# Where the states and the x transposes of a cross-attention and maxout-FFN kernel stand in the order of work

## The chip, the cores and the metric

The kernel runs on one core of a Trainium2 chip. The metric is device time in microseconds (us). Five runs of the kernel before gave a median of 156.76 us (156.15 to 157.01).

A core has five engines with their own instruction queues: TensorE (PE: matmuls and transposes into psum), VectorE (DVE), ScalarE (ACT), GpSimd (POOL) and SyncE (SP, which here only issues DMAs). Each executes its queue strictly in the order written; semaphores make one wait for another.

## The reference

```python
def _attn_ref(x, state):                  # x: (8, 8, 512, 64), state: (8, 8, 32, 64)
    scores = scale * np.matmul(x, state.transpose(0, 1, 3, 2))
    a = softmax(scores)                    # over the 32 states
    xread = np.matmul(a, state)
    scores2 = scale * np.matmul(state, x.transpose(0, 1, 3, 2))
    a2 = softmax(scores2)                  # over the 512 rows of x
    sread = np.matmul(a2, x)
    return np.concatenate([xread, sread], axis=2)

x = attn_out.transpose(0, 2, 1, 3).reshape(B * S, H * D)   # 4352 tokens of 512
h = np.maximum(np.maximum(x @ w1, x @ w2), x @ w3)         # 768 wide
out = h @ w_out
```

Every x row of a batch attends to the 32 states of its head, every state to the 512 rows; the concatenated result goes through a feed-forward net whose hidden layer is the maximum of three products.

## The kernel before, in words

Everything is in bf16 with fp32 accumulation. Instead of computing xread and then x @ w, the kernel multiplies the states of a batch by the weights first (G, by `g_cols`, `g_piece`, `g_front`, `g_back`); the hidden layer is then the softmax weights times G. For a batch b the steps are:

- x of the batch is loaded by a GpSimd DMA (`load_x`) and transposed to xT. For batches 0 to 2 that is done on PE in two halves of eight 128x128 transposes each (`x_transpose(b, g, copy)`, lines 157 to 167: transposes L164 into a psum tile, copied out to xT at L167 by the engine named). From batch 3 on one DMA transpose on SP's queue does it (`x_transpose_dma`, L171).
- `scores` (L185) multiplies xT by the states, which lie block by block in a tile `bds[k]` for the pair of batches 2k and 2k + 1; ScalarE takes the exp (L190, tile e). `softmax` sums and inverts on VectorE (L197, L199) and multiplies on GpSimd (L200, tile a).
- a is transposed to aT (on PE for batches 0 to 2, `a_transpose`, L211 and L212; later by DMA, L216).
- `sread` (L230) computes the second attention from e and x; its result is DMA-transposed into `ats` by `late_transposes` (L238). ats is read only in the last batch's iteration, by `s_maxout`.
- `x_maxout(b, m)` (L332) does one of six blocks of the hidden layer: three products of two matmuls each into three psum tiles; ScalarE copies the first (t0, L336), VectorE takes the maximum with the second (L339) and with the third (L340, tile ht). Each step frees one psum tile.
- `ffn_out(b, j)` (L370) multiplies by w_out, six matmuls; ScalarE copies out (L373); the output is stored by DMA (L382).

The state tile of a pair is made in three steps. `load_st` loads it (L58). `states_cast` (L135) casts it and doubles it into `st[k]`. `states(k, copy)` transposes it, on PE for the first two pairs (L142) and by a DMA on SP's queue for the others (L145, tile stT), and puts it into `bds[k]` by two copies (L148).

Psum is shared by two groups of buffers: tag "pw" (four buffers: the products of `x_maxout`, `ffn_out`, the transposes, `sread`, the short G pieces) and tag "two" (two larger ones: scores and G). A new tile waits for whoever last read the buffer that it gets.

The order of the work is written out by hand. The lines 391 to 470 are a first phase, in which batches 0 and 1 are worked on together and batch 2 is prepared. The loop at line 473 then does, for each batch b from 2 on, its six `x_maxout` blocks, and between them, in slots, the attention of batch b + 1 and the output of batch b - 1. In slot 2 of odd n = b + 1 the states of the next pair are transposed and placed (lines 480 and 481). In `g_cols` a copy can be deferred; it is then issued inside the next `x_maxout`, behind its t0.

The part of the first phase around the change, before it: the cast of pair 1 (line 444), the states of pair 1 and the x transposes of batch 2 (446 to 448), x_maxout(0, 5), g_cols of batch 1, x_maxout(1, 3), scores and softmax of batch 2 (449 to 453), the waiting ats transposes and the transpose of x of batch 3 (454, 455), output and G work, load_x(5), and the casts of pairs 2 and 3 (460 to 462).

Of the kernel before, what the change touches and what calls it, by code (L numbers as in the profile page):

```python
# [9 lines left out]
BF16 = mybir.dt.bfloat16  # L10
# [5 lines left out]
def kernel(  # L16
# [14 lines left out]
    nc = tc.nc  # L31

    B, H, S, D = x.shape
# [15 lines left out]
    data = ctx.enter_context(tc.tile_pool(name="data", bufs=1))  # L49
    wpool = ctx.enter_context(tc.tile_pool(name="weights", bufs=1))  # L50
    work = ctx.enter_context(tc.tile_pool(name="work", bufs=2))
    pp = ctx.enter_context(tc.tile_pool(name="pp", bufs=2, space=bass.MemoryType.PSUM))
    ctx.enter_context(tc.manual_schedule())
    dve, act, pool = nc.vector.tensor_copy, nc.scalar.copy, nc.gpsimd.tensor_copy
# [31 lines left out]
    ident = const.tile([128, 128], BF16, name="ident")  # L86
# [13 lines left out]
    def m_cols(t, m):  # L100
        c = [m0 <= m < m1 for m0, m1 in chunks].index(True)
        f = (m - chunks[c][0]) * 128
        return w_slices(t, c)[:, :, :, f:f + 128]
# [25 lines left out]
    def bd(b, h):  # L129
        return bds[b // 2][:, b % 2, h]  # L130

    st = [data.tile([128, 4, 2, D], BF16, name=f"st{k}") for k in range(B // 2)]

    def states_cast(k, cast):
        cast(out=st[k], in_=st_f[k].unsqueeze(2).to_broadcast((128, 4, 2, D)))  # L135

    def states(k, copy):

        if k < 2:
            p = pp.tile([128, 4, 128], BF16, tag="pw", bufs=4, name="pt")  # L140
            for t in range(4):
                nc.tensor.transpose(p[:, t, :], st[k][:, t].rearrange("p c d -> p (c d)"), ident)  # L142
        else:
            p = data.tile([128, 4, 128], BF16, name=f"stT{k}")
            nc.sync.dma_start_transpose(out=p, in_=st[k].rearrange("p t c d -> p (t c d)"))  # L145
        for c in range(2):
            r = slice(64 * c, 64 * c + 64)
            copy(out=bds[k][r, :, :, c, :].rearrange("p b h (q t) -> p (b h) q t", t=4),  # L148
                 in_=p[r].rearrange("p t (k q) -> p k q t", q=8))


    xT, e, a, aT, G, ht, osb = {}, {}, {}, {}, {}, {}, {}
# [1 line left out]
    def new(d, b, shape, name, bufs=2):  # L154
        d[b] = work.tile(shape, BF16, tag=name, bufs=bufs, name=name)

    def x_transpose(b, g, copy):

        if g == 0:
            new(xT, b, [128, H, 2, 128], "xT", bufs=3)  # L160
        p = pp.tile([128, HS, 2, 128], BF16, tag="pw", bufs=4, name="pxt")
        for s in range(HS):
            for jj in range(2):
                nc.tensor.transpose(  # L164
                    p[:, s, jj, :],
                    xv[b][:, 2 * s + g, 2 * jj:2 * jj + 2, :].rearrange("p j d -> p (j d)"), ident)
        copy(out=xT[b].rearrange("p (s g) j t -> p g s j t", g=2)[:, g], in_=p)  # L167
# [5 lines left out]
    def scores(b, g0, g1):  # L173
        n = g1 - g0
        if g0 == 0:
            new(e, b, [128, J, 2, HS, Ns], "e")
        if n == 2:
            p = pp.tile([128, J, n, HS, Ns], F32, tag="two", name="ps")
        else:
            p = pp.tile([128, J, n, HS, Ns], F32, tag="pw", bufs=4, name="psh")  # L180
        for jj in range(2):
            for g in range(g0, g1):
                for s in range(HS):
                    h = 2 * s + g
                    nc.tensor.matmul(  # L185
                        p[:, 2 * jj:2 * jj + 2, g - g0, s, :], xT[b][:, h, jj, :],
                        bd(b, h).rearrange("p c n -> p (c n)"),
                        start=(g == g0 and s == 0 and (n == 2 or jj == 0)),
                        stop=(g == g1 - 1 and s == HS - 1), skip_group_check=True)
        nc.scalar.activation(out=e[b][:, :, g0:g1], in_=p, func=AF.Exp, scale=scale)  # L190

    def softmax(b, g0, g1, mul):
        n = g1 - g0
        if g0 == 0:
            new(a, b, [128, J, 2, HS, Ns], "a")
        den = work.tile([128, J, n, HS], F32, tag=f"den{n}", name="den")
        nc.vector.reduce_sum(out=den, in_=e[b][:, :, g0:g1], axis=AX.X)  # L197
        rden = work.tile([128, J, n, HS], F32, tag=f"rden{n}", name="rden")
        nc.vector.reciprocal(out=rden, in_=den)  # L199
        mul(  # L200
            out=a[b][:, :, g0:g1].rearrange("p j g s n -> p j (g s) n"),
            in0=e[b][:, :, g0:g1].rearrange("p j g s n -> p j (g s) n"),
            in1=rden.rearrange("p j g s -> p j (g s)").unsqueeze(3).to_broadcast((128, J, n * HS, Ns)))
# [40 lines left out]
    def flush_copies():  # L244
        while copies_due:
            copies_due.pop(0)()
# [30 lines left out]
    def g_cols(b, ms, copies=(act, act), defer=(False, False)):  # L277
        flush_copies()
        for m, copy, wait in zip(ms, copies, defer):
            if m == 0:  # L280
                new(G, b, [128, 2, NM * 384], "G", bufs=3)
            p = pp.tile([128, 2, 512], F32, tag="two", name="pg")
            pv = p[:, :, 0:384].rearrange("p g (i f) -> p g i f", i=3)
            for s in range(HS):
                for g in range(2):
                    nc.tensor.matmul(  # L286
                        pv[32 * s:32 * s + 32, g], bd(b, 2 * s + g)[64 * g:64 * g + 64, g, :],
                        m_cols(w_sb, m)[64 * g:64 * g + 64, s],
                        start=True, stop=True, tile_position=(64 * g, 32 * s))

            def place(m=m, pv=pv, copy=copy):
                copy(out=m_cols(G[b], m), in_=pv)  # L292

            if wait:
                copies_due.append(place)
            else:
                place()
# [27 lines left out]
    def maxout(b, m, n, lhs, rhs, nk):  # L325
        if m == 0:
            new(ht, b, [128, NM, n], "ht", bufs=4)
        pw = []
        for i in range(3):
            p = pp.tile([128, 512], F32, tag="pw", bufs=4, name=f"pw{i}")  # L330
            for k in range(nk):
                nc.tensor.matmul(p[:, 0:n], lhs(i, k), rhs(k), start=(k == 0), stop=(k == nk - 1))  # L332
            pw.append(p)
        t0 = work.tile([128, 512], BF16, tag="t0", name="t0")
        t1 = work.tile([128, 512], BF16, tag="t1", name="t1")
        nc.scalar.copy(out=t0[:, 0:n], in_=pw[0][:, 0:n])  # L336
        if copies_due:
            copies_due.pop(0)()
        nc.vector.tensor_max(t1[:, 0:n], t0[:, 0:n], pw[1][:, 0:n])  # L339
        nc.vector.tensor_max(ht[b][:, m, :], t1[:, 0:n], pw[2][:, 0:n])  # L340

    def x_maxout(b, m):
        maxout(b, m, 512,
               lambda i, k: m_cols(G[b], m)[:, k, i],
               lambda k: aT[b][:, :, k, :], 2)
# [41 lines left out]
    def late_transposes():  # L387
        while late:
            late.pop(0)()
# [51 lines left out]
    x_maxout(0, 3)  # L441
    g_cols(0, (4, 5), defer=(False, True))
    x_maxout(1, 2)
    states_cast(1, pool)
    x_maxout(0, 4)
    states(1, act)
    x_transpose(2, 0, dve)
    x_transpose(2, 1, act)
    x_maxout(0, 5)
    g_cols(1, (4, 5), defer=(False, True))  # L450
    x_maxout(1, 3)
    scores(2, 0, 2)
    softmax(2, 0, 2, nc.gpsimd.tensor_mul)
    late_transposes()
    x_transpose_dma(3)
    ffn_out(0, 0)
# [2 lines left out]
    ffn_out(0, 1)  # L459
    load_x(5)  # L460
    for k in range(2, B // 2):
        states_cast(k, pool)
    x_maxout(1, 5)
    a_transpose(2, 0, act)
    a_transpose(2, 1, dve)
# [7 lines left out]
    for b in range(2, B):  # L473
        n = b + 1
        slots = [[] for _ in range(NM)]
        if n < B:
            slots[0].append(lambda: scores(n, 0, 2))
            slots[1].append(lambda: softmax(n, 0, 2, nc.gpsimd.tensor_mul))
            slots[2].append(lambda: a_transpose_dma(n))
            if n % 2 and n + 1 < B:  # L480
                slots[2].append(lambda: states((n + 1) // 2, pool))
            if n + 2 < B:
                slots[2].append(lambda: x_transpose_dma(n + 2))
            slots[5].append(late_transposes)
            if n + 3 < B:
                slots[0].append(lambda: load_x(n + 3))
        else:
            for m in range(NM):
                slots[m].append(lambda m=m: s_maxout(m))
        slots[1].append(lambda: g_back(b))  # L490
        if n < B:
            slots[4].append(lambda: sread(n))
            slots[4].append(lambda: g_front(n))
        for j, m in enumerate((1, 2, 4, 5)):
            slots[m].insert(0 if m > 2 else len(slots[m]), lambda j=j: ffn_out(b - 1, j))
        for m in range(NM):
            x_maxout(b, m)
            for f in slots[m]:
                f()
# [36 lines left out]
```

## Time and profile before

| | |
|---|---|
| profiled execution | 156.68 us, its span 154.8 us |
| PE busy | 146.3 us, 95% of the span |
| VectorE, ScalarE, GpSimd busy | 98.2, 93.9, 51.2 us |
| granted PE clock | full in all 40 slices |
| chain that ended last | PE 81%, ACT 6%, DMA 4%, POOL 3%, DVE 2% |
| costliest lines of the chain | L332 43%, L370 27% |
| GpSimd copies bd<-stT, L148 | 4 of 1.07 us; GpSimd waited 8.9 us in all for them |

In the profile's group lines stand the source line, the engine, the operation, the tile written and those read, the shape, the number of instructions, the busy time and the mean of one, and at last how long the engine stood idle before them and who ended that. In a timeline a row begins with its start, counted from the start of the span, and its length; rows of equal instructions are merged. In the chain of waits each row is a start, a length, and what the last-ending work was then held by.

### The profile page before, as it was taken

The page shows a single profiled execution, that of the slowest core. Times are in us where ns is not written, and L with a number is a line of the kernel's source. Part 1 is how long each engine was busy: PE and PEld are TensorE (multiplying, and loading weights), DVE is VectorE, ACT ScalarE, POOL GpSimd, SP SyncE. Part 2 cuts the span into 40 slices and gives each one's busy share as a digit, 9 for nine tenths or more (in the row PEclk, how much of TensorE's full clock was granted, in tenths as well). Part 3 has the DMA queues.
Part 4 walks back from the last instruction along what each step waited for, and adds up shares of the span by engine and source line. Part 5 has one row for each costly group of instructions (what it writes and reads, how often), then busy time and mean ns, then how long its engine had stood idle before and what let it go on. Part 6 is the DMA issues. An engine that isn't in the chain of part 4 may idle for free.

```text
span 154.8 us, 3467 instructions
## 1 busy us (share of the span) xinstructions
PE 146.3 (95%) x1373; PEld 72.5 (47%) x1389; DVE 98.2 (63%) x173; ACT 93.9 (61%) x145; POOL 51.2 (33%) x73
## 2 busy tenths in 40 slices
PE   6898999999999999999999999999999999999990
PEld 2455443544553445344534453445344556666450
DVE  4777958768617675767576757675767583565110
ACT  3275788897647656865686568656865637333340
POOL 8979793003731409160104250601060100100050
PEclk9999999999999999999999999999999999999999
DMA  3999999999299996989930893070307030110374
GB/s 119 206 180 188 195 197 165 239 201 171 112 130 126 269 198 153 251 112 238 114 135 0 161 225 135 2 207 8 135 12 196 16 132 0 68 70 0 140 239 168
DMA packets 36736, 21.72 MB, mean 140 GB/s; under 512 B 21968, under 2 KB 34384, under 8 KB 36720
## 3 DMA queue, kind: packets, MB, share of 16 engines
q0 software_dynamic: 17232, 15.08, 51.2%
q1 hardware_dynamic: 19344, 6.29, 23.0%
q8 instruction: 11, 0.18, 0.5%
q10 hardware_dynamic: 144, 0.13, 0.2%
q14 instruction: 5, 0.04, 0.1%
HBM read 15.20 MB, written 8.91 MB: 156 GB/s over the span
## 4 chain that ended last, share of the span: by engine, by line
PE 81%; ACT 6%; DMA 4%; POOL 3%; DVE 2%; issue 2%; POOLq 0%; ACTq 0%
PE pw L332 43%; PE po L370 27%; DMA w<-in_moe_w_dram 4%; PE pg L260 4%; PE psr L230 2%; ACT G L292 2%; POOL x L80 2%; PE ps L185 2%; ACT t L336 1%; ACT e L190 1%; PE pg L286 1%; POOL w L110 1%; PE ph L362 1%; DVE den L197 1%; PE pxt L164 1%
## 5 line engine op out<-in xcount | busy, mean ns | idle before, releaser
L332 PE MATMUL pw<-aT,G 128*128 128x512 bf16 x288 | 68.8, 379 | 0.7 <-ACT G L292 0.4
L339 DVE TENSOR_TENSOR t<-t,pw 128x512 bf16<-128x512 bf16 (+1 forms) x54 | 35.0, 649 | 30.8 <-ACT t L336 30.6
L370 PE MATMUL po<-wout,ht 128*128 128x512 bf16 x183 | 46.6, 379 | 0.9
L332 PEld LDWEIGHTS <-G 128*128 128x128 bf16 x288 | 27.1, 98 | 33.0 <-issue 2.7
L340 DVE TENSOR_TENSOR ht<-t,pw 128x512 bf16<-128x512 bf16 (+1 forms) x54 | 35.5, 658 | 6.0 <-DVE t L339 0.5
L373 ACT COPY osb<-po 128x512 f32<-128x512 f32 x33 | 19.3, 586 | 29.8 <-PE po L370 29.8
L336 ACT CAST t<-pw 128x512 bf16<-128x512 f32 (+1 forms) x54 | 30.5, 565 | 9.7 <-PE pw L332 9.0
L370 PEld LDWEIGHTS <-ht 128*128 128x128 bf16 x198 | 18.8, 98 | 23.8 <-issue 2.8
L200 POOL TENSOR_TENSOR a<-e,rden 128x1024 bf16<-128x1024 bf16 (+1 forms) x9 | 14.6, 1627 | 39.3 <-DVE rden L199 23.4
L267 ACT CAST G<-pg 128x1024 bf16<-128x1024 f32 x24 | 24.5, 1021 | 3.8 <-PE pg L260 3.2
L382 POOL DMA_DIRECT2D out_dram<-osb x14 | 8.0, 570 | 45.2 <-ACT osb L373 36.5
L197 DVE TENSOR_REDUCE den<-e 128x32 f32<-128x1024 bf16 (+1 forms) x10 | 9.9, 995 | 0.8 <-ACT e L190 0.8
L292 ACT CAST G<-pg 128x768 bf16<-128x768 f32 x11 | 8.7, 809 | 2.0 <-PE pg L286 2.0
L110 POOL DMA_DIRECT2D w<-in_moe_w_dram x12 | 9.1, 779 | 0.0
L332 PE MATMUL pw<-ats,w 128*128 128x256 bf16 x72 | 8.8, 273 | 0.0
L190 ACT ACTIVATE e<-ps 128x1024 bf16<-128x1024 f32 x6 | 6.1, 1024 | 3.8 <-PE ps L185 3.7
L332 PEld LDWEIGHTS <-w 128*128 128x128 bf16 x72 | 7.0, 98 | 2.1
L260 PE MATMUL pg<-w,bd 64*32 64x512 bf16 x192 | 7.5, 381 | 0.0
L126 PE MATMUL idle<-zero 128*128 128x512 bf16 x18 | 6.3, 480 | 1.2 <-DVE zero L85 1.2
L148 POOL COPY bd<-stT 64x512 bf16<-64x512 bf16 x4 | 4.3, 1071 | 9.0 <-DMA stT<-st 8.9
L185 PEld LDWEIGHTS <-xT 128*128 128x128 bf16 x128 | 4.9, 98 | 2.6 <-DVE xT L167 0.7
L70 POOL DMA_DIRECT2D x<-in_x_dram x6 | 5.4, 917 | 0.0
(54 smaller groups left out, 81.5 us busy)
## 6 DMA issues: line engine op xcount, KB each, us to landing
out_dram<-osb POOLq DMA_DIRECT2D x14, 512.0 KB, 3.1
x<-in_x_dram POOLq DMA_DIRECT2D x6, 512.0 KB, 9.6
w<-in_moe_w_dram POOLq DMA_DIRECT2D x6, 256.0 KB, 7.0
x<-in_x_dram POOLq DMA_DIRECT2D x3, 256.0 KB, 5.7
w<-in_moe_w_dram POOLq DMA_DIRECT2D x6, 128.0 KB, 6.6
wout<-in_moe_w_out_dram POOLq DMA_DIRECT2D x1, 768.0 KB, 10.8
x0f<-in_x_dram SPq DMA_DIRECT2D x1, 512.0 KB, 3.8
out_dram<-osb SPq DMA_DIRECT2D x1, 512.0 KB, 2.6
```

The costliest lines, as they stand in the source:

```text
L110: nc.gpsimd.dma_start(out=w_slices(w_sb, c)[:, :, i, :], in_=w[:, :, m0 * 128:m1 * 128])
L197: nc.vector.reduce_sum(out=den, in_=e[b][:, :, g0:g1], axis=AX.X)
L200: mul(out=a[b][:, :, g0:g1].rearrange("p j g s n -> p j (g s) n"), in0=e[b][:, :, g0:g1].rearrange("p j g s n -> p j (g s) n"), in1=rden.r ...
L260: nc.tensor.matmul(ps[g][32 * s:32 * s + 32], bd(b, 2 * s + g)[64 * g:64 * g + 64, g, :], w_sb[64 * g:64 * g + 64, s, c0:c1], start=True, ...
L267: copy(out=G[b][:, :, c0:c1], in_=p[:, :, 0:n])
L292: copy(out=m_cols(G[b], m), in_=pv)
L332: nc.tensor.matmul(p[:, 0:n], lhs(i, k), rhs(k), start=(k == 0), stop=(k == nk - 1))
L336: nc.scalar.copy(out=t0[:, 0:n], in_=pw[0][:, 0:n])
L339: nc.vector.tensor_max(t1[:, 0:n], t0[:, 0:n], pw[1][:, 0:n])
L340: nc.vector.tensor_max(ht[b][:, m, :], t1[:, 0:n], pw[2][:, 0:n])
L370: nc.tensor.matmul(p, ht[b][:, m, j * 128:(j + 1) * 128], wout_sb[:, m, :], start=(m == 0), stop=(m == NM - 1))
L373: act(out=o[:, j, :], in_=p)
```

## The change

- `states` is cut into `states_transpose(k, dma)` and `states_place(k, copy)`; `states(k, copy)` remains for pairs 0 and 1 and does both, on PE.
- The casts of pairs 2 and 3 (states of batches 4 to 7) stand right behind that of pair 1.
- Their DMA transposes are issued on SP's queue behind the softmax of batch 2, ahead of `late_transposes` and of the transpose of x of batch 3.
- Their placing copies on GpSimd stand where the casts were, behind load_x(5).
- The loop issues no states any more.
- The second half of the PE transposes of x of batch 2, with its ScalarE copy, moves behind x_maxout(0, 5) and g_cols(1, (4, 5)).

```diff
-    def states(k, copy):
-
-        if k < 2:
-            p = pp.tile([128, 4, 128], BF16, tag="pw", bufs=4, name="pt")
+    stT = {}
+
+    def states_transpose(k, dma):
+
+        if dma:
+            stT[k] = data.tile([128, 4, 128], BF16, name=f"stT{k}")
+            nc.sync.dma_start_transpose(out=stT[k], in_=st[k].rearrange("p t c d -> p (t c d)"))
+        else:
+            stT[k] = pp.tile([128, 4, 128], BF16, tag="pw", bufs=4, name="pt")
             for t in range(4):
-                nc.tensor.transpose(p[:, t, :], st[k][:, t].rearrange("p c d -> p (c d)"), ident)
-        else:
-            p = data.tile([128, 4, 128], BF16, name=f"stT{k}")
-            nc.sync.dma_start_transpose(out=p, in_=st[k].rearrange("p t c d -> p (t c d)"))
+                nc.tensor.transpose(stT[k][:, t, :], st[k][:, t].rearrange("p c d -> p (c d)"), ident)
+
+    def states_place(k, copy):
         for c in range(2):
             r = slice(64 * c, 64 * c + 64)
             copy(out=bds[k][r, :, :, c, :].rearrange("p b h (q t) -> p (b h) q t", t=4),
-                 in_=p[r].rearrange("p t (k q) -> p k q t", q=8))
+                 in_=stT[k][r].rearrange("p t (k q) -> p k q t", q=8))
+
+    def states(k, copy):
+        states_transpose(k, False)
+        states_place(k, copy)
...
     x_maxout(1, 2)
-    states_cast(1, pool)
+    for k in range(1, B // 2):
+        states_cast(k, pool)
     x_maxout(0, 4)
     states(1, act)
     x_transpose(2, 0, dve)
-    x_transpose(2, 1, act)
     x_maxout(0, 5)
     g_cols(1, (4, 5), defer=(False, True))
+    x_transpose(2, 1, act)
     x_maxout(1, 3)
     scores(2, 0, 2)
     softmax(2, 0, 2, nc.gpsimd.tensor_mul)
+    for k in range(2, B // 2):
+        states_transpose(k, True)
     late_transposes()
     x_transpose_dma(3)
...
     load_x(5)
     for k in range(2, B // 2):
-        states_cast(k, pool)
+        states_place(k, pool)
     x_maxout(1, 5)
...
             slots[2].append(lambda: a_transpose_dma(n))
-            if n % 2 and n + 1 < B:
-                slots[2].append(lambda: states((n + 1) // 2, pool))
             if n + 2 < B:
```

## The prediction

> **What bounds the kernel now.** I read four views in this order: the page's busy table, busy time by stretches cut at batch borders, the chain of work that ended last, and ScalarE's instructions in the stretch that the change rewrites.
>
> ```profile
> PE 146.3 (95%) x1373; PEld 72.5 (47%) x1389; DVE 98.2 (63%) x173; ACT 93.9 (61%) x145; POOL 51.2 (33%) x73
> ```
>
> The matrix engine is the bound on average; no other engine passes 63%. The average must be split, because the change works in one stage only. The stretches begin where the FFN of a batch starts (two columns matter: length and PE busy).
>
> ```profile
> 29.26:44.58 15.32, 14.73 (x163) 7.71 (x164) 10.32 (x19) 10.83 (x16) 4.60 (x5) 1.00 0.97 163
> 44.58:59.99 15.41, 15.31 (x147) 7.03 (x148) 10.49 (x18) 10.24 (x15) 5.11 (x5) 1.00 1.30 196
> 59.99:75.40 15.41, 15.30 (x148) 7.03 (x148) 10.72 (x19) 10.24 (x15) 4.87 (x6) 1.00 0.91 175
> 75.40:90.81 15.41, 15.30 (x148) 7.02 (x149) 10.72 (x19) 10.24 (x15) 5.13 (x5) 1.00 0.53 101
> 90.81:106.20 15.39, 15.29 (x147) 7.03 (x148) 10.70 (x19) 10.24 (x15) 2.99 (x3) 1.00 0.43 136
> ```
>
> The loop runs at 15.41, 15.41, 15.41 and 15.39 us per batch. The first and the third of these hold a state placement (states of batches 4 and 5, then 6 and 7), the others hold none, and they are equal: the placement costs the loop 0.00 to 0.02 us. Only the first phase has PE time to win: 15.32 - 14.73 = 0.59 us. There the chain of waits tells who sets the pace (start, us, what):
>
> ```profile
> 30.11 0.69 DVE ht L340
> 30.80 0.04 issue
> 30.84 1.46 PE pw L332 x6
> ...
> 33.35 0.59 ACT t L336
> 33.94 0.70 ACT G L292
> ...
> 34.71 1.03 ACT e L190
> 35.74 0.02 issue
> 35.77 1.23 DVE den L197
> ...
> 37.29 0.64 DVE t L339
> 37.93 0.04 issue
> 37.97 1.47 PE po L370 x6
> ```
>
> Two places, not one. PE waits near 30.5 for a psum buffer, which VectorE's second max frees at 30.80. From 33.35 to 37.97 the chain leaves PE: ScalarE's t0, its G copy and its exp of batch 2, then VectorE's row sum, reciprocal and max, which frees the buffer for ffn_out(0, 1). So ScalarE's order before that exp is the bound there:
>
> ```profile
> 29.69 1.17 ACT L148 COPY bd<-pt 64x512 bf16<-64x512 bf16 x2 [0.50 <-PE pt L142]
> 30.88 1.01 ACT L167 COPY xT<-pxt 128x1024 bf16<-128x1024 bf16 x1
> 31.79 0.59 ACT L336 CAST t<-pw 128x512 bf16<-128x512 f32 x1
> 32.66 0.80 ACT L292 CAST G<-pg 128x768 bf16<-128x768 f32 x1 [0.27 <-PE pg L286]
> 33.35 0.59 ACT L336 CAST t<-pw 128x512 bf16<-128x512 f32 x1
> 33.83 0.82 ACT L292 CAST G<-pg 128x768 bf16<-128x768 f32 x1
> 34.71 1.02 ACT L190 ACTIVATE e<-ps 128x1024 bf16<-128x1024 f32 x1
> ```
>
> The reader is to see that the xT copy of 1.01 us stands early, where ScalarE otherwise waits, and that from 32.66 to the exp ScalarE runs without a gap.
>
> **Part 1, states of batches 4 to 7 out of the loop.** Removed from the loop: two SP issues of 1.27 us, four GpSimd copies of 1.07 us, and 8.9 us in which GpSimd sat waiting for stT. None is on the path: the loop is PE's, equal with and without them. The placement was ready at 60.37 (58.18 + 2.19) for scores at 61.28, and at 90.21 for scores at 92.27 in the chain, so no wait existed. Gain 0.00, at most 0.02 us each, 0.04 in all.
>
> Added to the first phase, GpSimd: the casts (0.63 us each) move from 41.85 to behind the cast of batches 2 and 3, where GpSimd waits 13.0 us for rden. Their input is issued at 20.42 to 21.57 and lands 10.2 us later: casts end near 31.5 and 32.1, over 5 us before the softmax multiply at 37.53. Cost 0. The four copies stand behind load_x(5), which ends at 41.87: 4 x 1.07 = 4.3, less the 1.19 of casts that left, so GpSimd is free at 46.2 to 46.5. Queued behind them are the output issue (45.66 now) and load_x(6) (46.22 now), late by under 1 us. The output's buffer is rewritten by ffn_out(2, 0), whose copy is at 60.19; x of batch 6 is transposed at 70.44. The next multiply is at 51.28. Cost 0. GpSimd reads SBUF beside VectorE: in the present placement at 58.18 VectorE's max beside it takes 0.69, as elsewhere. Cost 0.
>
> Added, SP's queue: two transposes and, now behind them, two ats transposes that today run at 17.37, all ahead of the transpose of x of batch 3, today issued at 33.77 when its load lands. The working: first cast 31.5, then 2 x 1.27 = 34.05, then 2 x 1.1 = 36.3; there xT of batch 3 is issued, 2.5 us later than today. Such a transpose lands 5.0 to 10.2 us after its issue (five of them, median 6.1), so at 41.3 to 46.5; its reader, scores(3), is at 45.88 now and about 46.2 after. Cost: 0 at the median with 3.8 us in hand, 0.3 us at the slowest row. I take 0: the slowest row, issued at 44.03, had two output stores and two loads of x beside it, while around 40 us the DMA share of the page falls to 2 tenths.
>
> One row speaks against taking 0: an ats transpose issued at 19.38 beside loads landed only 6.8 us later, against 2.2 at best.
>
> The Trainium skill, "DMA: Bandwidth & Descriptors", section "Queues, rings and completion order", speaks against this part too: each DMA engine takes turns between the queues, a packet at a time. By that the early transposes and the loads of x of batches 3 and 4 would slow each other, and one would put the 0.3 us into the sum, by the trace's median row none.
>
> **Part 2, second half of the transposes of x of batch 2.** Nothing is removed or added: 8 transposes (0.46 us of PE) and the 1.01 us copy on ScalarE move behind x_maxout(0, 5) and g_cols(1, (4, 5)). With the buffers the program gives, step by step (ScalarE's next instruction starts 0.10 before the recorded end of the one before, as 33.35 against 32.66 + 0.80):
>
> - PE: first half ends 29.49 + 0.46 = 29.95. x_maxout(0, 5) now has three different releasers: VectorE's first max of (0, 4), at 30.00; the second max at 30.79, the one it waits for today; the state copies of ScalarE at 30.86. Its first pair of matmuls runs at 30.04, the second at 30.84, the third at 31.27, to 31.70. Today it ends at 30.84 + 1.29 = 32.13: 0.43 earlier, since a pair fills the old wait.
> - g_cols then 31.80 to 32.25 (0.10 and 0.45 as today), the moved half 32.25 to 32.71, x_maxout(1, 3) at 32.71, today 32.68. The 0.43 is paid back by 0.46. PE stands at +0.03.
> - ScalarE: state copies to 30.86; t0 of (0, 5) 30.76 to 31.35; then idle until the first G copy, 0.43 behind the start of g_cols as today: 32.23 to 33.03. Then the xT copy 32.93 to 33.94, t0 of (1, 3) 33.84 to 34.43, second G copy 34.33 to 35.15, exp at 35.05 to 35.15. Today 34.71. The scores themselves start at 34.00 and read the second half from 34.1, just behind the copy.
> - The exp is late by 0.34 to 0.44. VectorE's row sum follows it by 0.03 (its own max of (1, 3) would end at 35.95, before the exp ends at 36.1), then reciprocal, max, and the buffer of ffn_out(0, 1): 37.97 becomes 38.31 to 38.41. PE today arrives there at 37.87, so nothing absorbs it. Behind it everything up to the loop hangs on ffn_out(0, 1) and the loop has no slack.
>
> So +0.37 us, between 0.34 and 0.44. **Sum:** 0.00 + 0.00 + 0.37, against this execution's own 156.68 (span 154.8 and 1.88 around it): 157.05. The median of the runs shown, 156.76, is 0.08 above the profiled one, within their 156.15 to 157.01. I predict 157.05, +0.2%. About 0.5% (0.78 us) is what a measurement of this kernel can tell from no change; the forecast is inside it.
>
> **Rivals.** *Nothing comes of the move (156.7).* ScalarE may take the moved copy in time: it has 0.88 us free between 31.35 and 32.23. For: the scores are at the same time on PE. Against: the copy can't use the gap, since its transposes come after g_cols on PE; it stands between two instructions that were back to back.
>
> *The freed wait is kept (156.3).* PE's 0.35 us wait near 30.5 is gone, and if the exp were not the bound PE would keep it: 156.68 - 0.35 = 156.33. All of the stretch's 0.59 us of PE idling would give 156.09. For: a real wait goes. Against: the half that moved costs PE the same behind it, and the chain leaves PE at 33.35 already.
>
> *x of batch 3 comes late (up to 159.3).* With the ats issues at their slowest row (2.08 each) xT of batch 3 is issued at 31.5 + 2.54 + 4.16 = 38.2, and at the slowest landing, 10.2, it is there at 48.4; scores(3) then runs 2.6 us later than today's 45.88, and the loop passes that on: 159.3. It decides from a landing later than 46.2, and is slower by over 0.5% from 46.65. For: three queues of transposes in one file, and loads in flight until about 37. Against: 3.8 us in hand at the median, and the free DMA engines near 40.
>
> **How the numbers follow.** Forecast, +0.2 to +0.6 us: 0.60. Nothing comes of it: 0.18. Wait kept: 0.08. x of batch 3 late: 0.14, of which two thirds pass 0.5%. The spread of the runs around each adds a little on both sides. Range 156.2 to 158.0: from the kept wait, through the forecast with its 0.44 and the 0.3 of the slowest landing (157.4), to the late case's lower half; what is left out is the late case's upper part and the tail under the kept wait. Faster by over 0.5%: 0.06 (the 0.59 us of idling does not reach 0.78 by itself); within: 0.76; slower: 0.18.
>
> **What would show it.** In the changed profile: x_maxout(0, 5)'s first pair near 30.0 and the next near 30.84; ScalarE's xT copy between the two G copies near 32.9; the exp of batch 2 near 35.1 and ffn_out(0, 1) near 38.35; batch stretches still 15.4; no GpSimd wait for stT in the loop. Wrong if the exp starts before 34.9, if scores(3) waits for the DMA of xT, or if a batch stretch differs from 15.4 by over 0.1.

## The result, and the profile after

The changed kernel is slower by half a per cent: ratio 1.0047, 95% interval 1.0029 to 1.0064 (44 runs, median 157.92 us, against 79 runs of the kernel before, median 156.96). In time that is 0.74 us, between 0.46 and 1.00. I had forecast +0.37. The ratio leaves out executions that are over 1.5% above the fastest of their kernel (13 of the 44), which is why it is smaller than that of the two medians (1.006); the profiles of three experiments below (states alone, placing later, states with the extra load) are of such executions and are not read for their span.

The profiled execution of the changed kernel took 158.6 us, its span 156.8, 2.0 more than the one before. First the page of the changed kernel: busy times, the chain by line, and the group of x_maxout (at the end of its line: the idle time of PE just before these matmuls and who ended most of it).

```profile
PE 146.7 (94%) x1373; PEld 72.4 (46%) x1389; DVE 98.3 (63%) x173; ACT 93.7 (60%) x145; POOL 51.2 (33%) x73
...
PE pw L340 40%; PE po L378 24%; DMA aT<-a 5%; DMA w<-in_moe_w_dram 4%; PE pg L268 3%; PE ps L193 2%; PE psr L238 2%; POOL x L80 2%; ACT G L300 1%; POOL a L208 1%; ACT t L344 1%; PE pg L294 1%; PE pxt L172 1%; POOL w L110 1%; DVE ht L348 1%
...
L340 PE MATMUL pw<-aT,G 128*128 128x512 bf16 x288 | 68.9, 379 | 1.6 <-DMA aT<-a 0.9
```

PE's work is the same (146.7 against 146.3). New in the chain is `DMA aT<-a`, 5%: the transpose of a. The same cuts at batch borders as before, in the changed kernel:

```profile
29.03:44.68 15.65, 14.73 (x163) 7.68 (x164) 10.32 (x19) 10.63 (x16) 7.20 (x8) 1.00 1.27 173
44.68:61.15 16.47, 15.46 (x147) 6.96 (x148) 10.71 (x18) 10.82 (x16) 5.62 (x6) 1.00 1.30 187
61.15:76.56 15.41, 15.30 (x147) 7.02 (x150) 10.49 (x18) 9.75 (x14) 3.96 (x4) 1.00 0.94 180
76.56:91.97 15.41, 15.30 (x148) 7.02 (x149) 10.71 (x19) 10.24 (x15) 3.03 (x3) 1.00 0.48 112
```

The first phase grew from 15.32 to 15.65, +0.33. The loop's first batch grew from 15.41 to 16.47, +1.06; the two behind it did not move. Together with a start that was 0.23 shorter and 0.84 more behind the loop, where the last stores of this execution landed slowly (3.1 us after the last issue, 2.2 before), that is the 2.0.

The first phase, PE's timeline of the changed kernel:

```profile
29.03 0.39 PE L147 MATMUL pt<-ident,st 128*128 128x128 bf16 x4
...
29.82 0.59 PE L340 MATMUL pw<-aT,G 128*128 128x512 bf16 x2
30.62 1.02 PE L340 MATMUL pw<-aT,G 128*128 128x512 bf16 x4 [0.20 <-DVE ht L348]
31.57 0.52 PE L294 MATMUL pg<-w,bd 64*32 64x384 bf16 x16
32.02 0.62 PE L172 MATMUL pxt<-ident,x 128*128 128x128 bf16 x8
32.48 1.46 PE L340 MATMUL pw<-aT,G 128*128 128x512 bf16 x6
...
38.07 1.46 PE L378 MATMUL po<-wout,ht 128*128 128x512 bf16 x6 [0.41 <-DVE t L347]
```

and ScalarE's, to be laid beside the one in the prediction:

```profile
32.00 0.80 ACT L300 CAST G<-pg 128x768 bf16<-128x768 f32 x1 [0.76 <-PE pg L294]
32.69 1.02 ACT L175 COPY xT<-pxt 128x1024 bf16<-128x1024 bf16 x1
33.60 0.61 ACT L344 CAST t<-pw 128x512 bf16<-128x512 f32 x1
34.07 0.83 ACT L300 CAST G<-pg 128x768 bf16<-128x768 f32 x1
34.76 1.07 ACT L198 ACTIVATE e<-ps 128x1024 bf16<-128x1024 f32 x1
```

Counted from the state transposes (29.03 here, 29.26 before), ffn_out(0, 1) comes after 9.04 us; it was 8.71. PE now waits 0.41 us for VectorE's max there. The first pair of x_maxout(0, 5) runs at 29.82, the second at 30.62, and x_maxout(1, 3) at 32.48: all within 0.02 of the times worked out, less the 0.23.

The loop's first batch. SP's queue of the changed kernel, then GpSimd's, then the chain there:

```profile
53.34 1.25 SPq L224 DMA_TRANSPOSE aT<-a  x1
54.76 6.01 SPq L179 DMA_TRANSPOSE xT<-x  x1
```

```profile
51.41 1.90 POOL L208 TENSOR_TENSOR a<-e,rden 128x1024 bf16<-128x1024 bf16 x1 [3.60 <-DVE rden L207]
53.36 0.63 POOL L390 DMA_DIRECT2D out_dram<-osb  x1
61.17 0.55 POOL L390 DMA_DIRECT2D out_dram<-osb  x1 [7.18 <-ACT osb L381]
```

```profile
51.41 1.91 POOL a L208
53.32 0.02 issue
53.34 7.68 DMA aT<-a
61.01 0.14 issue
61.15 1.46 PE pw L340 x6
```

The transpose of a of batch 3 and the first store of batch 1 are issued within 0.02 us of each other, and the transpose lands after 7.68 us. GpSimd's queue in the kernel before shows what has gone:

```profile
51.28 1.91 POOL L200 TENSOR_TENSOR a<-e,rden 128x1024 bf16<-128x1024 bf16 x1 [4.17 <-DVE rden L199]
58.18 2.19 POOL L148 COPY bd<-stT 64x512 bf16<-64x512 bf16 x2 [4.99 <-DMA stT<-st]
60.32 1.31 POOL L382 DMA_DIRECT2D out_dram<-osb  x2
```

These are the issue of aT's transpose and the matmuls that read aT, in the kernel before too:

```profile
53.22 1.25 SPq L216 DMA_TRANSPOSE aT<-a  x1
59.99 1.46 PE L332 MATMUL pw<-aT,G 128*128 128x512 bf16 x6
```

There GpSimd stood 4.99 us waiting for stT and then copied, and both stores of batch 1 left at 60.32, after aT had landed (4.4 us after its issue, at 57.6, and 2.4 us before PE read it). The idle wait that I had booked at nothing kept the store away from the transpose.

### The profile page after: what moved, and what is told of

Same layout as the page of the kernel before. It is cut to its first block, busy times and chain, and to the rows that moved or that the text cites. A ratio compares the mean times of both kernels' runs of the same rounds, so it can differ in the third digit from the quotient of the medians.

```text
span 156.8 us, 3468 instructions
## 1 busy us (share of the span) xinstructions
PE 146.7 (94%) x1373; PEld 72.4 (46%) x1389; DVE 98.3 (63%) x173; ACT 93.7 (60%) x145; POOL 51.2 (33%) x73
## 4 chain that ended last, share of the span: by engine, by line
PE 75%; DMA 9%; ACT 5%; POOL 4%; DVE 3%; issue 2%; POOLq 0%; DVEq 0%; ACTq 0%
PE pw L340 40%; PE po L378 24%; DMA aT<-a 5%; DMA w<-in_moe_w_dram 4%; PE pg L268 3%; PE ps L193 2%; PE psr L238 2%; POOL x L80 2%; ACT G L300 1%; POOL a L208 1%; ACT t L344 1%; PE pg L294 1%; PE pxt L172 1%; POOL w L110 1%; DVE ht L348 1%
## 5 line engine op out<-in xcount | busy, mean ns | idle before, releaser
L344 ACT CAST t<-pw 128x512 bf16<-128x512 f32 (+1 forms) x54 | 30.5, 565 | 10.7 <-PE pw L340 9.9
L208 POOL TENSOR_TENSOR a<-e,rden 128x1024 bf16<-128x1024 bf16 (+1 forms) x9 | 14.6, 1627 | 31.2 <-ACT t L344 15.4
L126 PE MATMUL idle<-zero 128*128 128x512 bf16 x18 | 6.8, 514 | 1.2 <-DVE zero L85 1.2
L238 PE MATMUL psr<-x,e 128*32 128x128 bf16 x256 | 5.0, 220 | 0.1
```

The source lines that it names most:

```text
L208: mul(out=a[b][:, :, g0:g1].rearrange("p j g s n -> p j (g s) n"), in0=e[b][:, :, g0:g1].rearrange("p j g s n -> p j (g s) n"), in1=rden.r ...
```

## The experiments

A ratio is against the kernel before. "9.04 or 8.71" below is the distance from the state transposes to ffn_out(0, 1) on PE.

**1. The x half alone.** In the kernel before:

```diff
-    x_transpose(2, 1, act)
     x_maxout(0, 5)
     g_cols(1, (4, 5), defer=(False, True))
+    x_transpose(2, 1, act)
```

> The kernel before with the x half moved and nothing else. Theory (two causes: ScalarE's order in the first phase, 0.33 us in the profile after; and the transpose of a of batch 3 landing late beside a store that GpSimd now issues early, 0.9 us of PE wait in that profile): the exp of batch 2 is late by 0.3 to 0.4 us against the start of the state transposes on PE, ffn_out(0, 1) follows 9.04 us behind that start instead of 8.71, PE doesn't wait for aT of batch 3, total +0.3 to +0.4 us, ratio 1.002. Rival (all of the +0.7 us is the first phase, the wait for aT is this one execution's): ratio 1.004 to 1.005 already here. Rival (the first phase cost nothing, all is DMA): ratio 1.000.

Measured: 9.04, aT landed 3.9 us after its issue, no wait for it; ratio 1.003 (0.9993 to 1.0067). PE's waits from 30 us on are the new one and one of 0.2 us that the kernel before has too:

```profile
PE po L370 <- DVE t L339: 0.4, 1, 0.4
PE pw L332 <- DVE ht L340: 0.2, 1, 0.2
```

The x half costs its 0.33 us by itself. The interval is too wide to tell 1.002 from 1.000 or 1.005; the trace tells it.

**2. The states alone.** The kernel after with the x half put back where it was.

> The kernel after with the x half put back: only the states are moved. Theory: ffn_out(0, 1) is back at 8.71 us behind the start of the state transposes; GpSimd still issues the first store of batch 1 right behind the multiply of batch 3, near 53.3 us, aT of batch 3 lands 7 to 8 us after its issue and PE waits 0 to 1 us for it; ratio 1.001 to 1.005. Rival (first phase alone): ratio 1.000 and no wait for aT.

Measured: 8.71 again; the store goes out beside aT (54.43 and 54.40), aT lands after 8.7 us, PE waits 1.9; ratio 1.0047 (1.0007 to 1.0087). So the state move costs time without the x half, and the first-phase loss is the x half's alone.

**3. After, batch 1 stored in one piece.**

```diff
+        if b == 1:
+            if j == 3:
+                nc.gpsimd.dma_start(out=rows, in_=o)
+            return
         if j == 1 or j == 3 or j0 == j:
```

> The kernel after, with batch 1 stored by one DMA behind its last copy instead of two halves, so that no store is issued beside the transpose of a of batch 3. Theory: aT of batch 3 lands 4 to 6 us after its issue near 53.3, PE doesn't wait for it; the first phase keeps its 0.33 us; ratio 1.002. Rival (the loads of x and the transpose of x of batch 4, which ended 1.75 and 2.35 us later than before, make aT late, and not the store): aT lands at 60.5 or later all the same, PE waits, ratio 1.004 to 1.005.

Measured: 9.04; aT after 4.7 us, no wait for it, although load_x(6) is issued as late as in the kernel after; ratio 1.0033 (0.9999 to 1.0068). But load_x(6) landed 10.2 us after its issue here and 12.1 in the profile after, so these two profiles alone don't part the store from a load that lands late.

**4. Before, with the store early.** `states` takes a third argument that parts its two halves: the placing copies come one slot later, the DMA transposes where they were. So the store leaves ahead of GpSimd's wait for stT:

```diff
...
-                slots[2].append(lambda: states((n + 1) // 2, pool))
+                slots[2].append(lambda: states((n + 1) // 2, pool, 1))
+                slots[3].append(lambda: states((n + 1) // 2, pool, 2))
```

> The kernel before with the placing copies of the states one slot later (the DMA transposes where they were): GpSimd issues the first store of batch 1 right behind the multiply of batch 3, near 53.2, and waits for stT behind it. Nothing else moves. Theory: aT of batch 3 lands later than its 4.4 us of before, by 1 us or more, and PE may wait for it by up to 0.5 us near 60; ratio 1.000 to 1.004. Rival (the late loads): aT lands as before, at 57 to 58, ratio 1.000.

Measured: ratio 1.0145 (1.0086 to 1.0204), which is 2.3 us (1.3 to 3.2), far above both. aT of batch 3 lands after 5.3 us, later than 4.4 by 0.9, and PE doesn't wait for it. The loss is elsewhere:

```profile
PE ps L192 <- POOL bd L155: 1.4, 1, 1.4
```

Beside the store of the other odd batch the state transpose of the last pair took 6.0 us to land (2.6 before), GpSimd placed it late, and the scores of batch 6 waited. I had not foreseen that. It shows the same sensitivity in another transfer: a store issued next to a DMA transpose that is soon needed. It also shows that the early store alone need not make PE wait for aT: my mechanism was not complete.

**5. Both undone.** States out of the loop, x half back, batch 1 in one store.

> The kernel after with both suspected causes undone: the x half put back, and batch 1 stored by one DMA behind its last copy; the states stay out of the loop. Theory: ffn_out(0, 1) follows 8.71 us behind the start of the state transposes, aT of batch 3 lands 4 to 5 us after its issue, no PE wait for it; ratio 1.000 (0.997 to 1.003). If something else of the change costs time, the ratio stays at 1.002 or more.

Measured: 8.71, ratio 1.0001 (0.9964 to 1.0039). But in its profile aT took 7.6 us and PE waited 0.8 with no store beside it. In that execution the transfers were slow already before: load_x(6) landed 13.3 us after its issue, against 10.2 in experiment 3. So a wait for aT also comes without the store beside it, where load_x(6) lands late enough.

**6. The copies behind load_x(6).** After, with the placing copies behind the second store of batch 0 and load_x(6), which is then issued as early as before.

```diff
-    for k in range(2, B // 2):
-        states_place(k, pool)
...
                 slots[0].append(lambda: load_x(n + 3))
+            if b < 4:
+                slots[0].append(lambda: states_place(b, pool))
```

> The kernel after with the placing copies behind the second store of batch 0 and load_x(6), those of the last pair one batch later: load_x(6) is issued about 0.9 us earlier, against the start of the state transposes, as in the kernel before. The store beside aT of batch 3 stays. Theory (the store needs only the transpose of x of batch 5 beside it): aT still lands 7 us or more after its issue, PE waits 0.5 to 2 us, ratio 1.004 to 1.008. Rival (it takes the late load_x(6) as well): aT lands in 5 to 6 us, no wait, ratio 1.002.

Measured: aT after 10.5 us, PE waits 3.7; ratio 1.014 (1.0055 to 1.0226). A late issue of load_x(6) is not needed for the wait. In this profile load_x(6) took 14.9 us to land, the longest without the extra load below, and behind the wait PE ran at half its clock for a while (see experiments 9 to 11). Why the load took so long here is not shown.

**7. The transpose of x of batch 5 later.** After, with it behind the ats transpose of batch 3.

> The kernel after with the transpose of x of batch 5 issued behind the ats transpose of batch 3, near 59 us, and no longer right behind the transpose of a of batch 3. Store and load_x(6) as in the kernel after. Theory (it takes both, the store and the big transpose): aT lands in 5 to 6 us, PE doesn't wait, ratio 1.002. Rival (the store alone is enough): aT lands 7 us or more after its issue and PE waits, ratio 1.004 or more.

Measured: aT after 6.6 us, just inside what PE leaves it, no wait in the profile; ratio 1.0039 (0.9994 to 1.0085). It decides nothing: the kernel after itself can be as quick, as the next experiment shows.

**8. After again, unchanged.**

> The kernel after unchanged, a second look. Theory: ffn_out(0, 1) again 9.04 us behind the start of the state transposes; aT of batch 3 again lands 7 to 9 us after its issue, PE waits for it. Rival (the wait was an accident of one execution): aT lands in under 6 us and PE doesn't wait.

Measured: 9.03, the store beside aT as before, and aT after 5.5 us. PE's waits from 30 us on:

```profile
PE po L378 <- DVE t L347: 0.4, 1, 0.4
PE pw L340 <- DVE ht L348: 0.2, 1, 0.2
```

The first-phase wait is there again, the wait for aT is not; the run took 156.39 us. So the theory as I had put it falls: the store does not always bring the wait. What it may do is take tolerance away. PE reaches the matmuls that read aT 6.8 us after its issue (53.22 to 59.99 in the kernel before); with the store aT needs 5.3 to 6.6 where PE doesn't wait (experiments 4, 7 and 8), without it 3.9 to 4.7 in all but experiment 5.

**9, 10, 11. A disturbance in every execution.** Three kernels got the same additional load of 512 KB, which nobody reads, on ScalarE's queue near 41 us; all have the first phase of before.

```diff
     a_transpose(2, 1, dve)
+    extra = data.tile([128, HS, J * D], F32, name="extra")
+    nc.scalar.dma_start(out=extra, in_=x_heads(7, 0)[1])
     sread(2)
```

The kernel before with it:

> The kernel before with one more load of 512 KB, whose result nobody reads, issued by ScalarE near 42 us, to make the transfers of 42 to 58 us slow in every execution (in those looked at so far they were slow in some and not in others, and the wait for aT of batch 3 came with that). Theory (the change makes the kernel less tolerant: with the placing copies ahead of load_x(6) that load is issued 0.9 us later, and a store is issued beside aT): here load_x(6) lands 2 to 3 us later than in the kernel before, aT of batch 3 lands 5 to 6.7 us after its issue, inside the 6.8 us that PE leaves it, no wait; ratio 1.000 to 1.002. Rival (the waits came from slow executions alone, whatever the kernel): the wait for aT appears here as in the two kernels of this call with the same load.

States moved:

> Only the states moved (x half as before), with the same extra load. Theory: aT of batch 3 lands 8 to 10 us after its issue, PE waits 1.5 to 3 us for it; ratio 1.010 to 1.020. Rival (slow executions alone): the same wait as in the kernel before with the load.

States moved, batch 1 in one store:

> As the second of this call (states moved, extra load), with batch 1 stored in one piece behind its last copy, so that no store lies beside aT. Theory: between the other two; aT lands 6.5 to 8 us after its issue, PE waits 0 to 1.2 us; ratio 1.001 to 1.008. If the store is all of the lost tolerance, it is as the first.

PE's waits (total, times, longest) in the kernel before with the load, where aT of batch 3 lands 8.5 us after its issue:

```profile
PE pw L332 <- DMA aT<-a: 2.4, 2, 2.0
PE ps L185 <- POOL bd L148: 1.2, 1, 1.2
```

with the states moved, where it lands after 12.0:

```profile
PE pw L340 <- DMA aT<-a: 5.5, 1, 5.5
```

and with one store, after 8.8:

```profile
PE pw L340 <- DMA aT<-a: 2.3, 1, 2.3
```

The ratios are 1.0264 (1.0202 to 1.0325) for the first and 1.0199 (1.0114 to 1.0285) for the third; for the second there is none. The lowest of six runs each were 160.05, 162.58 and 159.06 us (mean granted clock 0.994, 0.979 and 0.995). The load was stronger than I had meant: the kernel before waits too, also for a state placement that only it still has in the loop. But the order is plain, in the lowest runs and in the profiles, one of each kernel: with a store beside it aT comes last, with the store held back it is as good (8.8) as in the kernel before (8.5). The later issue of load_x(6), which the second and the third kernel share, is at most the 0.3 left over. Of the 3.2 us between 8.8 and 12.0, though, some 2.2 are load_x(6) itself, which landed 17.0 us after its issue in the second and 14.8 in the third; whether the store did that too is not shown.

A long wait costs more than the wait. These are the six matmuls behind it in the third kernel and in the first:

```profile
62.50 2.72 PE L340 MATMUL pw<-aT,G 128*128 128x512 bf16 x6 [2.29 <-DMA aT<-a]
62.07 1.46 PE L332 MATMUL pw<-aT,G 128*128 128x512 bf16 x6 [1.96 <-DMA aT<-a]
```

Behind 2.29 us without work PE's granted clock was 0.50 of full from 62.5 to 65.0 us, and the matmuls took 2.72 us in place of 1.46; behind 1.96 us it stayed full. It fell to 0.50 as well behind the waits of 3.7 us (experiment 6) and 5.5 us (states moved, with the load), and stayed full behind 0.9 and 1.9 us (the kernel after, and experiment 2). Each time the slow matmuls added 1.7 to 2.1 us to the wait.

**12. Scores of batch 2 earlier.** Would taking the exp out of the chain gain what the x half lost? In the kernel before:

```diff
-    g_cols(1, (4, 5), defer=(False, True))
-    x_maxout(1, 3)
     scores(2, 0, 2)
     softmax(2, 0, 2, nc.gpsimd.tensor_mul)
+    g_cols(1, (4,))
+    x_maxout(1, 3)
+    g_cols(1, (5,))
```

> The kernel before with scores and softmax of batch 2 ahead of g_cols(1, (4, 5)), whose two blocks are set on both sides of x_maxout(1, 3): the exp of batch 2 leaves the chain that held ffn_out(0, 1). Theory (ScalarE's order before that exp sets the pace of the first phase): the exp starts near 3.5 us behind the start of the state transposes instead of 5.45, and ffn_out(0, 1) 8.4 to 8.6 us behind it instead of 8.71; ratio 0.998, too little for the timing to tell. Rival (PE is the bound there): 8.71 as before.

Measured: the exp stands 3.60 us behind the state transposes, and ffn_out(0, 1) 8.84, not less than 8.71; ratio 1.0004 (0.997 to 1.0038). The chain now runs through PE alone:

```profile
31.05 1.46 PE pw L332 x6
32.50 0.47 PE ps L185 x16
32.97 0.29 PE pg L286 x8
33.25 1.40 PE pw L332 x6
34.66 0.29 PE pg L286 x8
34.94 1.40 PE po L370 x6
36.34 1.36 PE pw L332 x6
37.71 0.56 PE pg L260 x16
38.26 0.11 PE pgs L260 x8
38.37 1.42 PE po L370 x6
```

The rival holds, more or less: PE was right behind ScalarE's chain all the time, 0.10 us (37.87 against 37.97). The chain had left PE, but nothing was to be won by shortening it, while lengthening it by 0.28 us (the exp 5.73 us behind the state transposes in the kernel after, 5.45 in the kernel before) cost 0.33.

**The profiles side by side.** load_x(6) is issued 6.4 to 7.3 us ahead of the transpose of a of batch 3 and is still in flight when that is issued. In us:

| profile | load_x(6) landed after its issue | aT landed after its issue | aT landed behind load_x(6) |
|---|---|---|---|
| *no store beside aT* | | | |
| before | 10.5 | 4.4 | 1.0 |
| 1, x half alone | 10.0 | 3.9 | 1.0 |
| 12, scores earlier | 10.5 | 4.4 | 1.0 |
| 3, one store | 10.2 | 4.7 | 0.9 |
| 5, both undone | 13.3 | 7.6 | 0.7 |
| 9, before, with the load | 15.1 | 8.5 | 0.7 |
| 11, one store, with the load | 14.8 | 8.8 | 0.7 |
| *a store beside aT* | | | |
| 4, early store | 9.6 | 5.3 | 2.7 |
| 8, after again | 9.6 | 5.5 | 2.3 |
| 7, x of batch 5 later | 10.7 | 6.6 | 2.3 |
| after | 12.1 | 7.7 | 2.0 |
| 2, states alone | 13.2 | 8.7 | 1.9 |
| 6, copies behind load_x(6) | 14.9 | 10.5 | 2.6 |
| 10, states moved, with the load | 17.0 | 12.0 | 1.8 |

Two things add up. The time at which load_x(6) lands spreads most, and aT lands close behind it in every profile: 0.7 to 1.0 us without a store, 1.8 to 2.7 with one. So the store adds 1 to 2 us to aT, and a late load_x(6) the rest. Why aT follows load_x(6) so closely, these profiles don't show. A rival stays untested: without the extra load, load_x(6) took 9.6 to 10.5 us in the four profiles with the state transposes in the loop and 9.6 to 14.9 in the seven with them moved, so the move may slow that load too, or the executions happened to be so.

## Why the prediction was half right

- *Part 2, the x half.* Right in mechanism and size: PE's steps within 0.02 us, the xT copy at 32.69 (32.93 less 0.23), the exp at 34.76 (34.82 to 34.92 worked out), and +0.33 us where I had 0.34 to 0.44. It is in every kernel with the moved half (9.03 or 9.04) and in none without (8.71, and 8.84 in experiment 12, which has an order of its own).
- *Part 1, SP's queue and x of batch 3.* Right: stT issued at 31.64 (worked out 31.5), xT of batch 3 at 36.90 (36.3), landed 5.0 us later, read at 45.98. That rival had the wrong transfer: what came late was aT. (In its sum, 48.4 is 2.5 us behind 45.88 and not 2.6; nothing else rests on that.)
- *Part 1, the loop.* This step failed: "8.9 us in which GpSimd sat waiting for stT. None is on the path ... Gain 0.00". I asked what the wait had cost and not what it had held back. Behind it on GpSimd's queue stood the first store of batch 1; freed, it is issued with aT of batch 3, on which PE has 2.4 us to spare (57.6 landed, 59.99 read). With the store at its side aT lands 1.8 to 2.7 us behind load_x(6) and not 0.7 to 1.0, and where load_x(6) lands late as well PE waits: 0.9 us in the profiled execution, 1.9 with the states alone, 0 in the second execution. I had written that an output and load_x(6) would be issued late by under 1 us at no cost, and both were, by 0.9 us against the state transposes; I had not seen that another output, the first store of batch 1, would be issued 7.0 us early (53.36, not 60.32). By my own sign, a batch stretch over 0.1 away from 15.4, this part was wrong: the loop's first took 16.47.
- *The sum.* Of 0.74 us (0.46 to 1.00) the x half is 0.33. The remaining 0.41 (0.13 to 0.67) fits a wait for aT that comes in some executions and not in others; no single interval here is narrow enough to show that share by itself, so its cause is argued from the profiles and not shown in the times. That the median of 157.92 us lies inside my 156.2 to 158.0 is luck as far as this part goes: I had set the upper end for an x of batch 3 that came late, and it came in time. Both undone, the ratio is 1.0001, with an interval that still allows 0.6 us each way.
- *Open:* how often the wait comes; why transfers between 42 and 58 us are slow in some executions (it happened in one without the store, and, without the extra load, in none of the four profiles of kernels whose state transposes stay in the loop); and why load_x(5) took 9.0 to 10.1 us in all profiles with the states moved and no extra load, and 8.4 to 8.8 in the four with the state transposes in the loop and no extra load.

## What to carry to other kernels

An idle engine off the path can be a brake: before a wait is taken away, list what stands behind it on that queue, DMA issues first, and look at which transfers will then lie side by side, with the reader of each and its slack. Where slack is a few microseconds of transfer time, one profile can't price it, since it holds in one execution and fails in the next, and a wait that grew past 2 us cost PE another 1.7 us or more here; a second execution, and a load added on purpose to all the variants compared, show who lost the tolerance. And a chain of waits that leaves the bound engine promises nothing by itself: see first how far behind that engine is.

## What was not expected of the hardware

A DMA transpose of one size (a of one batch) landed 3.9 to 10.5 us after its issue in these kernels, 12.0 with the added load, though its issue on SP took 1.25 us in most of them. It is much less steady than the compute engines, whose first-phase distance repeated to 0.01 us in all kernels of one order.
